# Loading the own probabilities in rows, and moving the second half of the sort matrices behind the first scores

## The chip, the core and the metric

The kernel runs on one core of one Trainium2 chip. The core has a matrix engine (PE; its weight loads are listed apart as PEld), a vector engine (DVE), a scalar engine (ACT), a general engine (POOL) and a sync engine (SP) that mostly issues transfers. Each engine works through its own list of instructions in order and waits on semaphores for the others. Transfers are carried by 16 shared DMA engines; this kernel issues them from SP's queue and from POOL's. PE writes its results to PSUM, from which DVE and ACT copy them into SBUF.

The metric is the device time of one execution in microseconds (us), as the median of several runs. A profile is one more execution, recorded instruction by instruction.

## The reference

Two stages are computed, one after the other. The first is Sinkhorn attention, with 4 batches, 8 heads, 768 tokens, head size 64, and 8 blocks of 96 tokens:

```python
P = sort_net                                  # (4, 8, 8, 8)
for _ in range(5):
    P = exp(P - max(P)); P = P / sum(P, rows); P = P / sum(P, columns)
k_sorted = einsum('bhij,bhjcd->bhicd', P, k in 8 blocks)     # v likewise
attn = softmax(q_block @ k_sorted_block.T / 8)               # within each block
x = attn @ v_sorted_block                                    # (3072, 512)
```

The second is a mixture of 4 experts over all 3072 rows, each row weighted by its own normalized probabilities:

```python
p = domain_probs / (domain_probs.sum(-1) + 1e-9)             # (3072, 4)
out = sum over e of p[:, e] * (relu(x @ w1[e]) @ w2[e])      # 512 -> 1024 -> 512
```

## The kernel before

The order of every engine's instructions is the order in which the program writes them down (a manual schedule), with planned slots later on. PSUM is handed out from two pools of two buffers each, `psM` and `psA`; a tile taken from a pool waits until the tile two takes earlier in that pool has been read.

The start goes like this. SP issues three transfers: `sn` (the sort logits), `p_in` (all probabilities) and `p_own` (the probabilities of the first 768 rows, as 128 partitions x 6 x 4, L171). POOL issues the first half of the queries, k and v of the first four heads and then of the other four, the first expert's first weights, builds the identity matrix `ident`, and some masks and constants. PE multiplies a dummy tile 84 times (`warm`, L276), so that its clock rises. DVE and ACT run the five Sinkhorn steps (L310 to L321), which are serial. In the fifth step PE transposes the first query halves (L288) and does 30 more dummy products.

The last step (L330) writes the sort matrices as `sn16` in two halves, output blocks 0 to 3 on DVE and 4 to 7 on POOL. `r_half(0)` (L342) spreads the first half over 128 partitions into the PSUM tile `ps_R` by four small products, and `build_PI0` (L353) multiplies it by a mask into patterns, four heads an instruction. With these, `mix_half` (L521) sorts and transposes k, or v, of the first batch; before its first use eight dummy products are made (`keep_warm`, L507). `mixed` (L532) copies the result out of PSUM, two blocks at a time. `h_s` multiplies queries by sorted keys and takes the exponential on ACT (L576, L582); `h_w` transposes sorted v (L548, L553); `h_a` is the product with v and the division (L593, L606, L607); `h_x` turns that into the experts' input `xT` (L624, L628); `group0` is the first expert's first layer (L704, L717). `r_half(1)` spreads the second half of the sort matrices, and the copy at L1402 puts both halves into `Rs`, from which POOL builds the patterns of the second half (`build_PI0(nc.gpsimd, 1, ...)`) and later those of the other batches. The relevant order is:

```python
mk0 = mix_half("k", 0, 0, psm, 8)
mixed("k", 0, mk0, 0, 2, act)
mv0 = mix_half("v", 0, 0, psa)
mixed("v", 0, mv0, 0, 2, vec)
r_half(1)
act(Rs.rearrange("p g (a i) -> p a g i", a=2), Rv.rearrange("p a i g -> p a g i"))
h_s(0, 0)
```

Here `vec` and `act` are the copies of DVE and of ACT. Somewhat later the second halves of k and v are mixed (`h_k`, `h_v`), each with one copy of 128 x 768 elements. `own_weights` (L263 to L266) normalizes `p_own` into `p_sb`, which weighs the first expert's output. `room` is a large tile that lies unused until the first expert's second layer.

From about 19 us the experts' products follow one another on PE, with the attention of the next batch in the slots between.

Of the kernel before, what the change touches and what calls it, by code (L numbers as in the profile page):

```python
# [10 lines left out]
F32 = mybir.dt.float32  # L11
# [7 lines left out]
def kernel(  # L19
# [11 lines left out]
    nc = tc.nc  # L31

    B, H, S, D = q.shape
# [4 lines left out]
    E = moe_w1.shape[0]  # L38
    FF = moe_w1.shape[2]
    P = 128  # L40
# [3 lines left out]
    R = BLK // CP  # L44
# [23 lines left out]
    def psa(shape, dtype, name):  # L68
        state["n"] += 1
        return psA.tile(shape, dtype, tag="ps", name=name)  # L70

    def psm(shape, dtype, name):
        return psM.tile(shape, dtype, tag="ps", name=name)
# [27 lines left out]
    room = const.tile([P, 4, Dm], F32, name="room")  # L101
# [5 lines left out]
    def load_natural(b, nm, qd, parts=1, between=None):  # L107
        src = {"k": k, "v": v}[nm]
        t = arena[:, ds(("k", "v").index(nm) * 2 * NW + qd * NW, NW)].rearrange("p (h r d) -> p h r d", h=4, r=R)
        natural[(b, nm, qd)] = t  # L110
        n = 4 // parts
        for m in range(0, 4, n):
            nc.gpsimd.dma_start(
                t[:, ds(m, n)].rearrange("p h r d -> p h (r d)"),
                src[b, ds(4 * qd + m, n)].rearrange("h (p r) d -> p h (r d)", r=R),
            )
            if m == 0 and between:
                between()
# [9 lines left out]
    def head(b, nm, h):  # L128
        return natural[(b, nm, h // 4)][:, h % 4, :, :]
# [20 lines left out]
    def load_half_queries(hf):  # L150
        for qd in range(2):
            nc.gpsimd.dma_start(
                q0[ds(64 * qd, 64), hf].rearrange("p h r d -> p h (r d)"), half_queries(qd, hf)
            )
# [7 lines left out]
    def p_part(at, n):  # L162
        return Tt[2].rearrange("p a f x -> p (a f x)")[:, ds(2 * at, 2 * n)].bitcast(F32)
# [4 lines left out]
    p_own = p_part(2 * E * NT + NT, R * E).rearrange("p (t e) -> p t e", e=E)  # L168
    own_den = p_part(2 * E * NT + NT + R * E, R).rearrange("p (t o) -> p t o", o=1)
    nc.sync.dma_start(p_in, moe_domain_probs.rearrange("(p t) e -> p t e", t=NT))  # L170
    nc.sync.dma_start(p_own, moe_domain_probs[0:S].rearrange("(t p) e -> p t e", p=P))  # L171
    load_half_queries(0)
    load_natural(0, "k", 0)


    ident = const.tile([P, P], F16, name="ident")
    make_identity(nc, ident)
    load_natural(0, "v", 0)
    load_natural(0, "k", 1)
    load_natural(0, "v", 1)  # L180
# [91 lines left out]
    def warm(n):  # L272
        ps = psM.tile([P, 4, P], F32, tag="ps", name=f"ps_w_{state['n']}")
        state["n"] += 1
        for m in range(n):
            nc.tensor.matmul(ps[:, m % 4, :], dummy, dummy, start=True, stop=True)  # L276
# [3 lines left out]
    def h_q(qd, hf, copy, ps=None):  # L280

        if ps is None:
            ps = psa([P, 2, R, 64], F16, f"ps_q_{qd}_{hf}")
        rows = ds(64 * qd, 64)
        for sg in range(2):
            for r in range(R):
                for hh in range(2):
                    nc.tensor.transpose(  # L288
                        ps[ds(D * hh, D), sg, r, :], q0[rows, hf, 2 * sg + hh, r, :], ident[rows, rows]
                    )  # L290
        if copy:
            copy(qT0[qd][:, :, hf], ps[:])
# [16 lines left out]
    for it in range(5):  # L309
        nc.scalar.activation(sn[:], sn[:], AF.Exp, bias=0.0, scale=1.0)  # L310
        if it == 4:
            for qd in range(2):
                h_q(qd, 0, nc.scalar.copy)
            warm(30)
        nc.vector.tensor_reduce(srow[:], sn[:], AX.X, ALU.add)
        nc.vector.reciprocal(srow[:], srow[:])
        nc.vector.tensor_tensor(sn[:], sn[:], srow[:].broadcast_to([GH, NB, NB]), ALU.mult)
        nc.vector.tensor_reduce(scol[:], sn[:].rearrange("p i j -> p j i"), AX.X, ALU.add)
        nc.vector.reciprocal(scol[:], scol[:])
        if it < 4:  # L320
            nc.vector.tensor_tensor(  # L321
                sn[:], sn[:],
                scol[:].rearrange("p j o -> p o j").broadcast_to([GH, NB, NB]),
                ALU.mult,
            )
            if it:
                next(p_steps)

    for a, eng in enumerate((nc.vector, nc.gpsimd)):
# [4 lines left out]
            ALU.mult,  # L334
        )

    ps_R = psM.tile([P, 2, 512], F32, tag="ps", name="ps_R")
    Rv = ps_R[:, :, 0:HB * GH].rearrange("p a (i g) -> p a i g", g=GH)

    def r_half(a):  # L340
        for i in range(HB):
            nc.tensor.matmul(  # L342
                Rv[:, a, i, :], sn16[:, a * HB + i, :, :].rearrange("g j c -> g (j c)"),
                ident[0:GH, 0:GH], start=True, stop=True,
            )
# [4 lines left out]
    Rs = const.tile([P, GH, NB], F16, name="Rs")  # L350

    def build_PI0(eng, a, h0, hn, src):
        eng.tensor_tensor(  # L353
            PI0[a][:, ds(h0, hn)],
            maskk[:, 0:HB * CP].rearrange("p (o i c) -> p o i c", o=1, c=CP).broadcast_to([P, hn, HB, CP]),
            src.rearrange("p g (i o) -> p g i o", o=1).broadcast_to([P, hn, HB, CP]),
            ALU.mult,
        )
# [18 lines left out]
            )  # L377

    r_half(0)
    for h0 in range(0, H, 4):  # L380
        build_PI0(nc.vector, 0, h0, 4, Rv[:, 0, :, ds(h0, 4)].rearrange("p i g -> p g i"))
    vec, act = nc.vector.tensor_copy, nc.scalar.copy


# [119 lines left out]
    def keep_warm(ps, n):  # L504

        for _ in range(n):
            nc.tensor.matmul(ps, dummy, dummy, start=True, stop=True)  # L507
# [3 lines left out]
    def mix_half(nm, qd, hf, pool, warm_up=0):  # L511

        ps = pool([P, 1024], F32, f"ps_m{nm}_{qd}_{hf}")
        keep_warm(ps[:, 0:P], warm_up)
        tails[(nm, qd, hf)] = ps[:, 2 * R * 64:1024].bitcast(F16).rearrange("p (n x) -> p n x", n=2)
        ps = ps[:, 0:2 * R * 64].rearrange("p (s r x) -> p s r x", s=2, r=R)
        for sg in range(2):
            for r in range(R):
                for hh in range(2):
                    h = 4 * qd + 2 * sg + hh  # L520
                    nc.tensor.matmul(  # L521
                        ps[ds(D * hh, D), sg, r, :],
                        head(0, nm, h)[:, r, :],
                        PI0[hf][:, h, :, :].rearrange("p i c -> p (i c)"),
                        start=True, stop=True,
                    )
        return ps

    def mixed(nm, qd, ps, i0, n, copy):

        dst = kTs[qd][:, 0:S] if nm == "k" else vT0[qd]
        copy(  # L532
            dst.rearrange("p (i x c) -> p x i c", i=HB, c=CP)[:, :, ds(i0, n)],
            ps.rearrange("p s r (i c) -> p (s r) i c", c=CP)[:, :, ds(i0, n)],
        )

    def h_k(qd, hf, copy, pool=psa):
        mixed("k", qd, mix_half("k", qd, hf, pool), 0, HB, copy)
# [27 lines left out]
    def h_s(qd, qq, ps=None):  # L566

        kT, ET = kTs[qd], ETs[2 * qd + qq % 2]
        if ps is None:
            ps = psa([P, 2, 512], F32, f"ps_s0_{qd}_{qq}")  # L570
        for n in range(4):
            for hh in range(2):
                sg, i = n // 2, 2 * (qq % 2) + n % 2

                m = BLK if 2 * i + sg == 3 else P
                nc.tensor.matmul(  # L576
                    ps[0:m, hh, ds(n * BLK, BLK)],
                    kT[ds(D * hh, D), ds((2 * i + sg) * BLK, m)],
                    qT0[qd][ds(D * hh, D), sg, qq // 2, :, ds((2 * (qq % 2) + n % 2) * CP, CP)],
                    start=True, stop=True,  # L580
                )
        nc.scalar.activation(  # L582
            ET[:, 0:S].rearrange("c (h x) -> c h x", h=2), ps[0:BLK, :, 0:HS],
            AF.Exp, bias=0.0, scale=SCALE,
        )
# [808 lines left out]
    ]  # L1394


    mk0 = mix_half("k", 0, 0, psm, 8)
    mixed("k", 0, mk0, 0, 2, act)
    mv0 = mix_half("v", 0, 0, psa)
    mixed("v", 0, mv0, 0, 2, vec)  # L1400
    r_half(1)
    act(Rs.rearrange("p g (a i) -> p a g i", a=2), Rv.rearrange("p a i g -> p a g i"))  # L1402
    h_s(0, 0)
    mixed("k", 0, mk0, 2, 2, act)
    load_half_queries(1)
    load_w2(0, 2)
# [33 lines left out]
    evacuate00()  # L1440
    group0(0, 1, 1, [2, 3])
    h_a(1, 1, ps_s11)
    h_k(0, 1, act)
    group0(1, 1, 0, [0, 1])
    h_x(1, vec, [1], ps_s11)
    group0(1, 1, 1, [0, 1])
# [131 lines left out]
```

## Time and profile before

| what | value |
|---|---|
| median of 3 runs | 358.63 us (358.15 to 358.74) |
| profiled execution, its own time | 358.21 us |
| span of that execution, first to last instruction | 356.3 us |
| PE busy | 350.4 us (98%) |
| DVE busy | 277.5 us (78%) |
| ACT busy | 170.1 us (48%) |
| POOL busy | 137.6 us (39%) |
| idle time of PE in the whole span | 5.9 us |
| granted clock of PE | 1.000, mean over the span |

Times in the profile count from the first instruction. A line such as L521 is a line of the kernel before; in the changed kernel the same code stands 3 to 9 lines further down. In lists of instructions "x24" is a count, "out<-in" names the tiles, "128x256" is partitions by elements, and the square brackets tell how long the engine sat idle before and who ended that. The chain that ended last gives start, length, and what it was.

### The profile page before, as it was taken

To read this page: it belongs to the slowest core of one execution; us is meant where nothing else is said; L and a number is where in the kernel's file an instruction comes from. 1 tells how busy PE (TensorE), PEld (TensorE's weight loads), DVE (VectorE), ACT (ScalarE), POOL (GpSimd) and SP (SyncE) were. 2 spreads that over 40 slices of the span, in tenths; PEclk is the share of its full clock that TensorE was granted. 3 is DMA by queue.
4 is the path that set the end of the run, shared out by engine and by line. 5 is a ranking of instruction groups with operands and counts; after the bars stand their busy time and mean duration, and the time that the engine had idled before them with its cause. 6 is when DMAs were issued, how large, how long until landed. Compare 5 with 4: busy or idle time off the path is not lost.

```text
span 356.3 us, 9511 instructions
## 1 busy us (share of the span) xinstructions
PE 350.4 (98%) x3948; PEld 305.5 (86%) x3948; DVE 277.5 (78%) x555; ACT 170.1 (48%) x302; POOL 137.6 (39%) x154
## 2 busy tenths in 40 slices
PE   8899999999999999999999999999999999999996
PEld 8686857888888888988899888888888888888886
DVE  5766787779798687778879988896678886588963
ACT  2653330452425445368847259830288611598301
POOL 8766112466022420000626318840068800188400
PEclk9999999999999999999999999999999999999999
DMA  8999999999999999743995410005200014100021
GB/s 104 203 205 230 212 209 194 207 195 167 195 180 166 195 116 203 138 88 44 180 205 91 107 74 0 2 1 136 78 26 3 2 37 141 62 0 2 0 75 46
DMA packets 74762, 40.26 MB, mean 113 GB/s; under 512 B 41568, under 2 KB 70496, under 8 KB 74720
## 3 DMA queue, kind: packets, MB, share of 16 engines
q0 software_dynamic: 38720, 19.93, 43.2%
q1 hardware_dynamic: 35856, 19.67, 27.2%
q8 instruction: 31, 0.51, 0.6%
q14 instruction: 11, 0.09, 0.1%
q10 hardware_dynamic: 144, 0.07, 0.1%
HBM read 41.88 MB, written 6.34 MB: 135 GB/s over the span
## 4 chain that ended last, share of the span: by engine, by line
PE 95%; DVE 3%; issue 0%; DMA 0%; ACT 0%; DVEq 0%
PE ps_h L815 18%; PE ps_Q L1296 18%; PE ps_p L799 12%; PE ps_X L1153 10%; PE ps_Z L1153 7%; PE ps_Q L1153 7%; PE ps_Z L1296 6%; PE ps_h L704 3%; PE ps_o L741 3%; PE ps_p L860 3%; PE ps_a L479 2%; PE ps_s L444 2%; PE ps_k L425 1%; PE ps_v L391 1%; PE ps_mv L521 1%; PE ps_a L593 0%
## 5 line engine op out<-in xcount | busy, mean ns | idle before, releaser
L815 PE MATMUL ps_h<-xT,w 128*128 128x256 f16 x576 | 67.5, 273 | 0.0
L815 PEld LDWEIGHTS <-w 128*128 128x128 f16 x576 | 55.2, 98 | 7.3
L821 DVE SCALAR_TENSOR_TENSOR Hb<-ps_h,pb 128x1024 f16<-128x1024 f32 x34 | 41.5, 1223 | 17.8 <-PE ps_h L815 17.6
L1153 PEld LDWEIGHTS <-w 128*128 128x128 f16 x480 | 43.6, 98 | 4.7
L1166 POOL TENSOR_TENSOR arena<-tmp,pb 128x512 f16<-128x512 f32 x12 | 15.2, 1276 | 65.7 <-PE ps_Z L1153 49.8
L1296 PEld LDWEIGHTS <-Hb 128*128 128x128 f16 x320 | 31.1, 98 | 3.5
L1165 ACT ACTIVATE tmp<-tmp 128x512 f32<-128x512 f32 x46 | 29.0, 632 | 3.9 <-DVE tmp L1203 3.9
L1296 PEld LDWEIGHTS <-Sb 128*128 128x128 f16 x304 | 28.2, 98 | 3.0
L1153 PEld LDWEIGHTS <-arena 128*128 128x128 f16 x312 | 27.7, 98 | 2.8
L451 ACT ACTIVATE ET<-ps_s 96x768 f16<-96x768 f32 x24 | 18.1, 802 | 25.2 <-PE ps_s L444 25.0
L434 ACT CAST kT<-ps_k 64x384 f16<-64x384 f32 x48 | 22.7, 473 | 13.3 <-PE ps_k L425 12.3
L126 POOL DMA_DIRECT2D arena<-in_q_dram x24 | 19.9, 842 | 20.8 <-DMA q_ring<-arena 17.7
L1153 PE MATMUL ps_X<-ET,arena 128*128 128x256 f16 x168 | 25.2, 272 | 0.0
L1296 PE MATMUL ps_Q<-w,Hb 128*128 128x256 f16 x192 | 24.6, 273 | 0.0
L799 PEld LDWEIGHTS <-Hb 128*128 128x128 f16 x232 | 21.9, 98 | 3.0
L1159 DVE SCALAR_TENSOR_TENSOR Hb<-ps_X,pb 128x512 f16<-128x512 f32 x27 | 18.7, 692 | 7.0 <-PE ps_X L1153 7.0
L1173 ACT COPY ps_X<-ps_Z 128x512 f32<-128x512 f32 x27 | 15.4, 571 | 17.8 <-PE ps_Z L1153 17.8
L1153 PE MATMUL ps_Z<-xT,w 128*128 128x256 f16 (+1 forms) x176 | 22.5, 258 | 0.0
L785 DVE TENSOR_TENSOR Sb<-Hb 128x512 f16<-128x512 f16 x33 | 20.6, 646 | 0.0
L1180 ACT COPY tmp<-ps_X 128x512 f32<-128x512 f32 x26 | 15.2, 586 | 9.2 <-PE ps_X L1153 6.6
L1159 DVE SCALAR_TENSOR_TENSOR Hb<-ps_Z,pb 128x512 f16<-128x512 f32 x27 | 18.4, 683 | 1.3 <-PE ps_Z L1153 1.3
L1203 DVE TENSOR_TENSOR tmp<-ps_Q,tmp 128x512 f32<-128x512 f32 x26 | 17.7, 683 | 0.8 <-PE ps_Q L1153 0.8
(270 smaller groups left out, 744.3 us busy)
## 6 DMA issues: line engine op xcount, KB each, us to landing
w<-in_moe_w_dram POOLq DMA_DIRECT2D x4, 1024.0 KB, 27.2
w<-in_moe_w_dram POOLq DMA_DIRECT2D x6, 512.0 KB, 19.7
arena<-in_k_dram POOLq DMA_DIRECT2D x7, 384.0 KB, 7.6
arena<-in_v_dram POOLq DMA_DIRECT2D x7, 384.0 KB, 8.1
vs<-arena SPq DMA_DIRECT2D x36, 66.0 KB, 5.3
arena<-in_q_dram POOLq DMA_DIRECT2D x24, 96.0 KB, 7.5
out_dram<-ob SPq DMA_DIRECT2D x9, 256.0 KB, 2.0
pb<-p_dram SPq DMA_DIRECT2D x4, 512.0 KB, 5.8
```

The lines of the kernel that those rows point to most:

```text
L126: nc.gpsimd.dma_start(t[:, h // 2, :, h % 2, :], q[b, h].rearrange("(t p) d -> p t d", p=P))
L434: nc.scalar.copy(kT[ds(D * hh, D), r], pk[ds(D * r, D), hh].rearrange("p a (i c) -> p a i c", c=CP),)
L451: nc.scalar.activation(ETs[2 * (pr % 2) + hh][:, 0:S].rearrange("c (a x) -> c a x", a=2), pss[hh][0:BLK, :, 0:HS], AF.Exp, bias=0.0, scale ...
L785: tt(sm[0], blk(0, 1), blk(1, 1), ALU.add)
L799: nc.tensor.matmul(ps, lhs(e, f), Ts[e][rhs][:, f, :], start=(first and e == es[0] and f == 0), stop=(done and e == es[-1] and f == KH - 1 ...
L815: nc.tensor.matmul(ps[:, f, :], w1sb[e][:, kc, ds((4 * g + f) * P, P)], xT[:, kc, ds(2 * c * P, 2 * P)], start=(kc == 0), stop=(kc == NKC ...
L821: nc.vector.scalar_tensor_tensor(out=Hb[:, homes.get(e, e), ds(4 * g, 4), :], in0=ps[:], scalar=0.0, op0=ALU.max, in1=weights(e).broadcast ...
L1153: nc.tensor.matmul(dst[:, ds(f * cols, cols)], a[lhs][:, k, ds((f0 + f) * P, P)], t[rhs][:, k, :], start=(first and f == 0 and k == 0), st ...
L1159: nc.vector.scalar_tensor_tensor(out=home(i, j), in0=src.rearrange("p (f x) -> p f x", f=m), scalar=0.0, op0=ALU.max, in1=weight(j).broadc ...
L1165: nc.scalar.activation(src, src, AF.Relu, bias=0.0, scale=1.0)
L1203: tt(t12, Q, u2, ALU.add)
L1296: nc.tensor.matmul(ps, lhs(e, f), Ts[e][rhs][:, f, part], start=(first and e == 0 and f == 0), stop=(e == E - 1 and f == KH - 1), skip_gro ...
```

## The change

There are six edits.

1. The own probabilities come in as they lie in memory: 6 rows of 128 x 4 values, in six partitions of `room`. A 6x6 float32 identity is copied on POOL, ahead of the second load of `load_natural`. Four float32 products, one for each expert, turn the rows into the layout of `p_own`, and DVE copies them there.
2. The dummy products in the fifth Sinkhorn step are 14 instead of 30.
3. The first patterns are built in three instructions, of 2, 2 and 4 heads, instead of two of 4.
4. The dummy products ahead of the first mix are 4 instead of 8.
5. `h_s(0, 0)` comes ahead of `r_half(1)`, and the copy into `Rs` runs on DVE instead of ACT.
6. The second half of k of the first four heads is copied on ACT in three pieces, of 2, 1 and 1 blocks.

```diff
-    nc.sync.dma_start(p_own, moe_domain_probs[0:S].rearrange("(t p) e -> p t e", p=P))
+    own_rows = room[0:R, 1, :].rearrange("t (p e) -> t p e", e=E)
+    nc.sync.dma_start(own_rows, moe_domain_probs[0:S].rearrange("(t p) e -> t p e", p=P))
     load_half_queries(0)
     load_natural(0, "k", 0)
...
     make_identity(nc, ident)
+    ident32 = room[0:R, 0, 0:R]
+    nc.gpsimd.tensor_copy(ident32, ident[0:R, 0:R])
     load_natural(0, "v", 0)
...
-            warm(30)
+            warm(14)
...
+    ps_own = psm([P, E, R], F32, "ps_own")
+    for e in range(E):
+        nc.tensor.matmul(ps_own[:, e, :], own_rows[:, :, e], ident32, start=True, stop=True)
+    nc.vector.tensor_copy(p_own.rearrange("p t e -> p e t"), ps_own[:])
     ps_R = psM.tile([P, 2, 512], F32, tag="ps", name="ps_R")
...
     r_half(0)
-    for h0 in range(0, H, 4):
-        build_PI0(nc.vector, 0, h0, 4, Rv[:, 0, :, ds(h0, 4)].rearrange("p i g -> p g i"))
+    for h0, n in ((0, 2), (2, 2), (4, 4)):
+        build_PI0(nc.vector, 0, h0, n, Rv[:, 0, :, ds(h0, n)].rearrange("p i g -> p g i"))
...
-    mk0 = mix_half("k", 0, 0, psm, 8)
+    mk0 = mix_half("k", 0, 0, psm, 4)
     mixed("k", 0, mk0, 0, 2, act)
     mv0 = mix_half("v", 0, 0, psa)
     mixed("v", 0, mv0, 0, 2, vec)
+    h_s(0, 0)
     r_half(1)
-    act(Rs.rearrange("p g (a i) -> p a g i", a=2), Rv.rearrange("p a i g -> p a g i"))
-    h_s(0, 0)
+    vec(Rs.rearrange("p g (a i) -> p a g i", a=2), Rv.rearrange("p a i g -> p a g i"))
...
-    h_k(0, 1, act)
+    mk01 = mix_half("k", 0, 1, psa)
+    for i, n in ((0, 2), (2, 1), (3, 1)):
+        mixed("k", 0, mk01, i, n, act)
```

## The prediction

> **What bounds the kernel now.** I read the page's part 1 first (who is busy), then the chain of work that ended last (what the busy engine is made of and where it is not PE), then the timeline of the first 20 us, because every edit lies before 27 us. Page, part 1 and part 4:
>
> ```profile
> PE 350.4 (98%) x3948; PEld 305.5 (86%) x3948; DVE 277.5 (78%) x555; ACT 170.1 (48%) x302; POOL 137.6 (39%) x154
> ...
> PE 95%; DVE 3%; issue 0%; DMA 0%; ACT 0%; DVEq 0%
> ```
>
> PE is busy 350.4 of 356.3 us; the chain has 3% of DVE, and that is the start. Chain, first 45 us:
>
> ```profile
> 10.86 0.69 DVE sn L330
> 11.60 0.26 PE ps_R L342 x4
> 11.86 0.55 PE ps_mk L507 x8
> 12.45 0.57 PE ps_mk L521 x24
> 13.01 0.39 PE ps_mv L521 x24
> 13.43 0.57 DVE Sb L532
> 14.04 0.44 PE ps_mv L548 x4
> 14.57 0.42 DVE Sb L553
> 14.99 0.47 DVE Sb L532
> 15.51 0.42 PE ps_s L548 x4
> 15.94 0.28 PE ps_s L576 x8
> 16.21 0.52 PE ps_mv L521 x24
> 18.77 0.66 PE ps_h L704 x8
> ```
>
> Up to 11.6 us the serial Sinkhorn steps set the time, and the change leaves them alone. From 11.6 to 18.8 us PE and DVE pass one small piece to each other. From 18.77 on PE follows PE, so what is gained by then is kept unless a load is late. Timeline, what the moved parts cost today:
>
> ```profile
> 11.23 1.23 POOL L330 TENSOR_TENSOR sn<-sn,scol 32x512 f16<-32x512 f32 x1
> 11.97 0.75 DVE L353 TENSOR_TENSOR Sb<-maskk,ps_R 128x256 f16<-128x256 f16 x2 [0.43 <-PE ps_R L342]
> 13.65 0.37 ACT L1402 CAST Rs<-ps_R 128x256 f16<-128x256 f32 x1
> 13.97 0.81 ACT L582 ACTIVATE ET<-ps_s 96x768 f16<-96x768 f32 x1
> 14.57 0.42 DVE L553 COPY Sb<-ps_mv 96x512 f16<-96x512 f16 x1 [0.59 <-PE ps_mv L548]
> ```
>
> The last line matters most: DVE idles 0.59 us there, between 13.99 and 14.57.
>
> **1. Own probabilities in rows.** The third DMA on SP's queue keeps its place; it changes from 768 packets of 16 B (6 x 128 rows) to 6 rows of 2 KB. From 2.6 to 5.1 us the small packets share the engines with the first query halves (transfer queues of that stretch: packets, MB, share of 16 engines):
>
> ```profile
> q0 software_dynamic: 361, 0.27, 72.0%
> q1 hardware_dynamic: 794, 0.02, 25.7%
> ```
>
> So q1 takes 25.7% of 2.5 us, 0.64 us at most. The POOL loads reach 130 packets per half microsecond alone and 76, 127 and 98 in the three halves from 3.5 us: 89 packets short, 0.34 us, of which the first half is also ramp; without it 0.14 us. The landing events put k0 at 10.28, v0 at 12.25, k1 at 14.16 and v1 at 16.10 us, and v1's product starts its weights at 16.14. That load is as late as the chain. I take 0.14 us earlier landings (bounds 0 and 0.34): enough to let the chain advance, nothing by itself. The four w1_0 parts land at 17.44, 18.69, 19.94 and 21.42 and are used at 18.58, 19.93, 21.00 and 21.80, so they hold nothing if PE comes 0.14 earlier.
>
> On POOL a 6x6 copy now stands ahead of v0, k1, v1, w1_0, the masks, the memsets and the second half of L330. Nearest rows: a 128x48 memset 0.16, a 128x128 copy 0.29; I take 0.2. The loads behind it wait in a full queue (v0 is issued at 4.13 and starts to move about 8.5), so they lose nothing; L330 ends at 12.66 instead of 12.46, needed about 13.6 (step 3).
>
> On PE 16 warm-ups go (the 30 took 1.85 us, 62 ns each: 0.99 us) and four fp32 products come, each one instruction that loads its own weights. No fp32 product is in the trace. Below: L342's four small ones, 0.26 us together. Above: weights and product in series, 4 x (98 + 219 ns) = 1.27 us. I take 1.0, nearer to the end whose weights also have 128 columns. PE is then free at 8.51 + 14 x 0.062 + 1.0 = 10.4, 1.2 us before L330's first half ends at 11.55: cost nothing. On DVE a 128x24 copy follows L330; a 96x8 reciprocal takes 0.20, a 128x24 one 0.28. It fits the 0.43 us for which DVE waits on ps_R. No gain or loss.
>
> The Trainium skill ("FP8 and Floating Point Precision", TensorE Precision Notes) has true fp32 take four passes; by the 62 ns row that would be an estimate of 16 x 0.062 = 0.99 us, the same cover; no run here shows it.
>
> **2. First patterns in three, four warm-ups fewer.** Two 128x256 instructions of 0.417 us start 0.33 us apart; the first k product starts at 12.45, 0.06 after the first ends. With two heads 128 elements go, at that spacing's slope about 0.14 us (bounds 0.10 and 0.22): product at 12.31. The second piece starts 0.2 later and ends at 12.45; the 12 products before it take 12 x 16 ns, so they barely wait. The extra instruction costs DVE about 0.07 us, before the v copy that waits until 13.29. Keeping eight warm-ups would have held PE to 12.41; four end at 12.18. Gain 0.14.
>
> **3. Second half behind the first scores, its copy on DVE.** Today r_half(1) runs at 13.33 and the scores at 13.59, released by ACT's k copy (13.53). With step 2 that copy ends at 13.39, scores 13.44, r_half(1) ends 13.94, L548 at 13.90: nothing queued behind it is late, as it ends weights by 13.8. ACT loses a 0.37 us copy; the exponential starts at 13.82 instead of 13.97. DVE gets the copy: 128x384 takes 0.56 and 128x256 thus about 0.43 (bounds 0.37, 0.56), from 13.98 to 14.41. L553 behind it is ready at 14.43. Price 0 (bounds 0 and 0.13), covered by the 0.59 us idle. Reader of the sums on POOL: L353 at 17.16, which waited for its own queue until then.
>
> **4. k's second half copied in three.** One ACT copy of 0.82 us becomes 0.48 + 2 x about 0.31 = 1.10 (from 0.48 for 384 and 0.82 for 768 elements: 0.14 fixed). It ends at 24.9; ACT then idles 1.69 us until 26.32, PE refills that bank at 26.21. Price nothing.
>
> **Sum.** 0.14 us off the profiled execution (358.21: span 356.3 and 1.9 around it), 358.07. The median, 358.63, lies 0.42 above it; I carry the difference over: 358.49.
>
> **The rivals.**
> - *More than the sum (faster).* The 0.42 of the median may be v1 landing later than in the profiled execution, and go with the small packets; with step 2 at its upper bound 0.22 and landings 0.34 earlier, and 0.1 for executions where the clock rises late and 30 warm-ups overrun 11.55: 358.63 - 0.22 - 0.34 - 0.1 to - 0.42 - 0.22 - 0.1, 357.97 to 357.89. For it: the coincidence 16.10/16.14. Against: no wait on DMA is left on PE in this execution.
> - *The clock drops (slower).* PE's windows of 3.41 us counted from the rise of the clock at 5.04:
>
> ```profile
> 8.45:11.86 3.41, 2.17 (x46) 1.93 (x38) 2.71 (x11) 1.62 (x3) 3.19 (x16) 1.00 1.28 195
> 353.19:356.30 3.11, 0.24 (x5) 0.07 (x2) 0.29 (x1) 0.00 (x0) 0.00 (x0) 1.00 0.36 126
> ```
>
> The columns are length, then PE, PEld, DVE, ACT, POOL. 64% busy kept the clock full; after the last window with 7% it fell at 356.6. The change leaves 2.17 - 0.99 + 0.26 to 1.27 = 1.4 to 2.4 us, 42 to 72%, between the two. If it falls at 11.86 for one window, the chain's PE pieces of 0.57, 0.39 and 0.44 stretch by the ratio of warm-up spacings before and after 5.04 (96 to 54 ns): 1.40 x 0.78 = 1.1 us, 359.6. It decides if the limit lies above what is left. The Trainium skill ("TensorE: Matmul & The Clock Gate", Part 1) has the clock fall after an idle window of about 3.4 us; by that rule the gap of 1.2 us changes nothing.
> - *The fp32 products run long (slower).* Four passes each in series, 16 x 0.32 = 5.1 us, would end at 14.5. It decides above 2.2 us in all (0.54 each); at 0.8 each PE is 1.0 late: 359.5. Nothing in the trace speaks for it but the missing separate weight loads.
> - *DVE late in step 3.* The copy at 0.56 and r_half(1) 0.15 later: 0.28 lost, 0.14 gained, 358.8.
>
> **How the numbers follow.** Forecast 0.56 (own range 358.1 to 358.8), faster rival 0.19, DVE late 0.07, clock 0.10, fp32 0.08. A change under 0.2% (0.72 us) can hardly be told from none here. The forecast and the late DVE give same 0.63; the faster rival, counted as past the bound, 0.19; the two slower ones 0.18. The range goes from 357.85 to 359.3, which leaves out most of the two slower ones.
>
> **What would show it.** The k product's start (12.45) 0.14 earlier; ps_own done well before 11.5; the Rs copy on DVE inside the idle time before L553; v1's product before 16.1; full clock from 5 us on. Wrong if r_half(0) starts after 11.6, if 128x128 products in the first 16 us take twice their time, or if v1's load holds PE.

## The result and the profile after

The changed kernel takes 359.95 us (median; 359.11 to 360.87, 8 runs) against 358.45 us of the kernel before in the same comparison (358.04 to 359.75, 8 runs): a ratio of 1.004, 95% interval 1.0025 to 1.0055. It is slower, by 1.5 us. The forecast was 358.49 us, with a range of 357.85 to 359.3. The profiled execution took 360.01 us.

The page of the kernel after: the span, busy times, the row of the granted clock (tenths of full speed in 40 slices of 9 us) and the shares of the chain.

```profile
span 358.0 us, 9493 instructions
...
PE 353.0 (99%) x3936; PEld 307.7 (86%) x3936; DVE 278.3 (78%) x558; ACT 169.9 (47%) x303; POOL 137.8 (38%) x155
...
PEclk9699999999999999999999999999999999999999
...
PE 95%; DVE 3%; DMA 0%; issue 0%; ACT 0%; DVEq 0%
```

PE is busy 2.6 us longer with twelve instructions fewer. Part of that is the new fp32 products (2.03 us, for dummies that took less); the rest is products that have become slower, not more. The second digit of the clock is a 6. The windows of 3.41 us, counted from the rise of the clock at 4.79 us, say where (columns: length, then busy time and instructions of PE, PEld, DVE, ACT and POOL, the granted clock, the transfers' share, GB/s):

```profile
4.79:8.20 3.41, 3.41 (x93) 3.31 (x93) 2.83 (x14) 0.51 (x2) 3.41 (x6) 1.00 1.19 159
8.20:11.62 3.42, 3.11 (x40) 2.88 (x32) 2.97 (x13) 1.62 (x3) 3.20 (x16) 1.00 1.24 178
11.62:15.03 3.41, 3.24 (x71) 2.75 (x72) 1.91 (x7) 1.00 (x2) 3.01 (x4) 0.50 1.30 201
15.03:18.44 3.41, 3.41 (x74) 2.85 (x73) 1.94 (x6) 2.26 (x4) 2.45 (x3) 0.50 1.24 206
```

The clock is at half for two windows, 11.62 to 18.44 us, exactly the stretch in which PE and DVE hand each other small pieces. The window before the fall has rows on PE for 3.11 of 3.42 us. What these rows are, PE and DVE show in the timeline of the kernel after:

```profile
8.40 0.95 PE L279 MATMUL ps_w<-Hb 128*128 128x128 f16 x14
9.28 2.03 PE L342 MATMUL ps_own<-room 6*128 6x6 f32 x8
11.66 0.19 DVE L343 COPY T<-ps_own 128x24 f32<-128x24 f32 x1
11.79 0.28 PE L349 MATMUL ps_R<-ident,sn 32*128 32x32 f16 x4 [0.48 <-DVE sn L333]
```

The fourteen dummies, and then the fp32 products: each of the four is recorded as two loads and two products, 2.03 us in all. They end at 11.31, before the sort matrices are there, so nothing waits for them. The chain of the kernel after, from the first sort product on:

```profile
11.79 0.28 PE ps_R L349 x4
12.07 0.54 PE ps_mk L514 x4
12.61 0.78 PE ps_mk L528 x13
13.39 0.64 PE ps_mv L528 x12
...
14.69 0.66 PE ps_mv L555 x4
15.35 0.78 PE ps_mk L528 x12
```

Before, the same pieces were 0.57 (k), 0.39 (v) and 0.44 (the transposes of sorted v, now L555). Marks along the two timelines, us:

| mark (start) | before | after | stretch before | stretch after |
|---|---|---|---|---|
| `r_half(0)` | 11.60 | 11.79 | | |
| first product of `group0` | 18.61 | 20.25 | 7.01 | 8.46 |
| first product of the second layer (`ps_o`) | 27.76 | 29.82 | 9.15 | 9.57 |
| first product of the next first layer (L815) | 36.83 | 38.58 | 9.07 | 8.76 |
| span | 356.3 | 358.0 | | |

So there are two losses, 1.45 us in the stretch at half clock and 0.42 us in the stretch after it, and differences of 0.2 to 0.3 us in the other two (the start and the last stretch), which the experiments below put down to no edit.

### The profile page after: what moved, and what is told of

Its sections match the earlier page's. It is cut to its first block, busy times and chain, and to the rows that moved or that the text cites. A ratio compares the mean times of both kernels' runs of the same rounds, so it can differ in the third digit from the quotient of the medians.

```text
span 358.0 us, 9493 instructions
## 1 busy us (share of the span) xinstructions
PE 353.0 (99%) x3936; PEld 307.7 (86%) x3936; DVE 278.3 (78%) x558; ACT 169.9 (47%) x303; POOL 137.8 (38%) x155
## 4 chain that ended last, share of the span: by engine, by line
PE 95%; DVE 3%; DMA 0%; issue 0%; ACT 0%; DVEq 0%
PE ps_h L822 18%; PE ps_Q L1303 18%; PE ps_p L806 12%; PE ps_X L1160 10%; PE ps_Z L1160 7%; PE ps_Q L1160 7%; PE ps_Z L1303 6%; PE ps_o L748 3%; PE ps_h L711 3%; PE ps_p L867 3%; PE ps_a L486 2%; PE ps_s L451 2%; PE ps_k L432 1%; PE ps_v L398 1%; PE ps_mk L528 1%; PE ps_mv L528 1%
```

## The experiments

The clock's mean over the span counts the windows lost: one window of 3.41 us at half clock is 3.41 / 356.3 / 2 = 0.005 of the mean, so 0.995, 0.99 and 0.986 are one, two and three. The eight executions of the kernel after lost one (359.11, 359.25, 359.55), two (359.9, 360.01, 360.02) or three (360.79, 360.87). None kept the clock.

### Are the sixteen dummies the cause?

Two theories. Clock: the sixteen dummies that go kept the clock up; the kernel before without them is as slow. Path: the fp32 products, the reordering or the copies hold the chain. Four kernels separate them. The changed kernel with thirty dummies:

```diff
-            warm(14)
+            warm(30)
```

> The changed kernel with the 30 dummy products of the kernel before in place of 14; all else as changed. Theory (the clock): the window before 11.6 us has enough products that count, so the mean granted clock goes back to about 1.000; but dummies (1.85 us) and the four float32 products (2.03 us) together end near 12.3 us, so r_half(0) starts 0.5 to 0.7 us late: about 359.0 us, 0.1 to 0.2% over the kernel before. Rival (the float32 products, or edits 3 to 6, cost the time themselves): the clock does not matter, and the time is that of the changed kernel plus 0.5 us or more, 360.4.

The kernel before with fourteen:

```diff
-            warm(30)
+            warm(14)
```

> The kernel before with 14 dummy products in the fifth Sinkhorn step instead of 30, nothing else. Theory (the clock): the 16 missing dummies are what let the clock drop, so it drops here too for one to three windows in most executions (mean clock 0.986 to 0.995): 359.3 to 360.0 us. Rival (the float32 products cause the loss): the clock stays at 1.000 and the time at 358.4.

The changed kernel without edits 1 and 2:

```diff
-    own_rows = room[0:R, 1, :].rearrange("t (p e) -> t p e", e=E)
-    nc.sync.dma_start(own_rows, moe_domain_probs[0:S].rearrange("(t p) e -> t p e", p=P))
+    nc.sync.dma_start(p_own, moe_domain_probs[0:S].rearrange("(t p) e -> p t e", p=P))
...
-    nc.gpsimd.tensor_copy(ident32, ident[0:R, 0:R])
...
-            warm(14)
+            warm(30)
...
-        nc.tensor.matmul(ps_own[:, e, :], own_rows[:, :, e], ident32, start=True, stop=True)
-    nc.vector.tensor_copy(p_own.rearrange("p t e -> p e t"), ps_own[:])
```

> The changed kernel with the own probabilities loaded as before, no float32 products, and 30 dummies: edits 3 to 6 alone. Theory (the clock alone makes the loss): clock 1.000, and the 0.14 us of the prediction's sum is gained, 358.3 us, at most 0.1% off. Rival (the moved copy on DVE or the three pieces cost the time): 358.8 us or more with a full clock.

And edits 1 and 2 alone, on the kernel before, which are these lines the other way round, with 14 dummies:

> The kernel before with edits 1 and 2 alone: rows, float32 products, 14 dummies. Theory (the clock): the whole loss is here, clock 0.986 to 0.995, 359.5 to 360.3 us. Rival (edits 3 to 6): 358.4 to 358.7 us at a full clock.

Measured, beside 358.15 us of the kernel before (34 runs, 33 of them at full clock with a median of 358.13):

| kernel | median us | ratio, 95% interval | executions with 0, 1, 2, 3 windows lost |
|---|---|---|---|
| changed, thirty dummies | 359.58 | 1.0042 (1.0017 to 1.0067) | 6, 4, 2, 0 |
| before, fourteen dummies | 359.36 | 1.0035 (1.002 to 1.005) | 0, 6, 2, 4 |
| edits 3 to 6, thirty dummies | 359.16 | 1.0032 (1.0011 to 1.0052) | 9, 3, 0, 0 |
| edits 1 and 2 | 359.65 | 1.0039 (1.0024 to 1.0053) | 0, 6, 2, 3 |

The second row is the main finding. One number changed, 30 to 14, every execution lost full clock, and the kernel before became as slow as the changed one: the interval holds the changed kernel's 1.004. Its executions also price a window: 358.13 with none, then medians of 358.94, 359.77 and 360.63 with one, two and three, so 0.81 to 0.86 us a window. The windows of that kernel from the rise of its clock:

```profile
5.75:9.16 3.41, 3.41 (x96) 3.26 (x95) 2.67 (x15) 0.51 (x2) 3.41 (x6) 1.00 1.17 152
9.16:12.58 3.42, 1.39 (x24) 1.09 (x22) 2.67 (x11) 1.62 (x3) 3.20 (x14) 1.00 1.26 192
12.58:15.99 3.41, 3.37 (x88) 3.00 (x88) 1.33 (x5) 1.98 (x4) 2.19 (x5) 0.50 1.29 203
```

With 1.39 us of rows on PE (41%) the next window is at half. Edits 1 and 2 add 2 us of fp32 products to the same fourteen dummies, and still all eleven executions fell: these products do not keep the clock.

At equal numbers of lost windows the changed kernel (359.25, 360.01, 360.83) lies 0.2 to 0.3 us above the kernel before with fourteen dummies. That is all that the other edits add to the missing dummies, which are enough by themselves for the other 1.2 us of the median. They are enough, but not the only way to lose the clock, for two rows missed their expectations. With the thirty back the changed kernel still lost windows in half of its executions; the last two runs take that up. And edits 3 to 6 lost a window in 3 of 12, where full clock was expected; their nine executions at full clock have a median of 358.68, with three of them between 360.06 and 361.85, for which no run has a cause.

### The smaller edits, at full clock

Four kernels stand on the kernel before: edits 3 and 4, edit 5, and edits 3, 5 and 6 with 30 and with 46 dummies. Only the first of them has four warm-ups ahead of the first mix, the others eight. Edits 3 and 4:

```diff
-    for h0 in range(0, H, 4):
-        build_PI0(nc.vector, 0, h0, 4, Rv[:, 0, :, ds(h0, 4)].rearrange("p i g -> p g i"))
+    for h0, n in ((0, 2), (2, 2), (4, 4)):
+        build_PI0(nc.vector, 0, h0, n, Rv[:, 0, :, ds(h0, n)].rearrange("p i g -> p g i"))
...
-    mk0 = mix_half("k", 0, 0, psm, 8)
+    mk0 = mix_half("k", 0, 0, psm, 4)
```

> The kernel before with edits 3 and 4 alone: patterns in 2, 2 and 4 heads, 4 dummies ahead of the first k product instead of 8; 30 dummies in the fifth step. Theory (the clock counts products that fill the array): with 4 dummies fewer some executions lose a window of the clock, as in edits 3 to 6 together (3 of 12 at 0.995 there); best time 358.0 or a little below, median 358.4 to 358.8. Rival (edit 5 or 6 is what loses): clock 1.000 throughout, median 358.0 to 358.2.

Edit 5:

```diff
+    h_s(0, 0)
     r_half(1)
-    act(Rs.rearrange("p g (a i) -> p a g i", a=2), Rv.rearrange("p a i g -> p a g i"))
-    h_s(0, 0)
+    vec(Rs.rearrange("p g (a i) -> p a g i", a=2), Rv.rearrange("p a i g -> p a g i"))
```

> The kernel before with edit 5 alone: first scores ahead of r_half(1), the copy into Rs on DVE; 8 and 30 dummies. Theory (the clock, with edit 4 as the reason for what edits 3 to 6 lose): no difference, 358.0 to 358.2 us, clock 1.000. Rival (DVE's copy holds the product behind it): 358.4 us or more at a full clock.

Edits 3, 5 and 6 together:

> Edits 3, 5 and 6 with 8 and 30 dummies as before. Theory (the clock): no lost windows, and of the 0.14 us only what eight dummies leave (they end at 12.41 in the kernel before, the first pattern would be ready at 12.31): 358.0 to 358.15 us. Rival (the order or the three pieces cost time themselves): 358.4 us or more, with slow executions at a full clock.

The same with 46 dummies:

```diff
-            warm(30)
+            warm(46)
```

> As the edits 3, 5 and 6, with 46 dummies in the fifth step instead of 30, so that they fill the time until the sort matrices are ready (8.5 + 46 x 0.062 = 11.35 us). Theory (the clock): the window that the change emptied is fuller than before; no execution loses a window, the slowest lie nearer to the fastest, median 358.0 to 358.1 us. Rival (dummies overrun in executions whose clock rises late): median 358.3 us or more.

| kernel | median us (before: 358.36) | ratio, 95% interval | windows lost |
|---|---|---|---|
| edits 3 and 4 | 358.28 | 1.0008 (0.9992 to 1.0025) | in 2 of 12 |
| edit 5 | 358.61 | 1.001 (0.9999 to 1.002) | in none of 12 |
| edits 3, 5 and 6 | 358.41 | 1.0003 (0.9991 to 1.0015) | in 1 of 11 |
| edits 3, 5 and 6, 46 dummies | 360.49 | 1.0058 (1.0039 to 1.0077) | in none of 6 |

The kernel before itself lies 0.2 us higher here than in the first comparison, so the expectations, given in microseconds, are best read by the ratios.

Edit 3 does what it is for: the first k product starts 0.72 us after `r_half(0)` instead of 0.85, and `group0` 6.89 us after it instead of 7.01. A gain of 0.12 us is under what the time can tell. Edit 4 adds little to it: with edits 3, 5 and 6 and all eight dummies the k product starts 0.74 us after `r_half(0)`.

Edit 5 has a wait that the prediction did not name. Chain of the kernel with edit 5 alone:

```profile
14.14 0.21 PE ps_R L342 x4
14.35 0.02 issue
14.37 0.44 DVE Rs L1403
14.81 0.04 issue
14.85 0.57 PE ps_mk L521 x24
15.42 0.36 PE ps_a L593 x8
```

The second mix of k takes the PSUM buffer of `ps_R`, so it does not start before DVE has copied `ps_R` (14.81, start at 14.85). It starts 3.04 us after `r_half(0)`, before 2.80. Some of the 0.24 us is made up at the next waits: the first product of `group0` comes 7.06 us after `r_half(0)`, before 7.01.

The last row missed its expectation by 2 us at full clock, although the dummies did not delay `r_half(0)` (11.82). In its profile PE waits for nothing that the profile shows ("issue") at two places; these waits from 15 to 50 us:

```profile
PE ps_w L548 <- issue: 0.9, 1, 0.9
PE ps_a L593 <- issue: 0.3, 1, 0.3
```

Between 150 and 200 us PE also waits 0.8 and 0.4 us for loads. The kernel before has no such wait of PE above 0.2 us in its profile. With 22 dummies in place of 30 (below) there was one "issue" of 0.60 us at 14.1. But with edits 3, 5 and 6 and 30 dummies, a list of PE as long as before, there was one too, of 0.57 us at 13.92, in an execution of 359.23 us. So the length alone does not decide. Counted in the traces, all these waits lie at the same places of PE's list: ahead of its 224th product (these two kernels, and edit 1 alone, below), its 352nd (46 dummies, and edit 1 alone) and its 608th (46 dummies, and the changed kernel with 30 and 8). An edit changes which product stands there; what is late was not settled, nor why most executions profiled show no such wait.

### Where the 0.42 us after the half clock come from

The stretch from `group0` to `ps_o` takes 9.15 or 9.16 us in the kernel before and with edits 3 and 4, with edit 5, with fourteen dummies and with edits 1 and 2, but 9.34 to 9.38 with edits 3, 5 and 6 (with or without edit 4, and with 46 dummies), and 9.56 to 9.58 in the changed kernel, with whatever dummies. Edit 6 is in all the long ones. So is something else: one, two or three more instructions in DVE's list (edits 1, 3 and 5 add one each). Two kernels separate these, edits 3 and 5 without 6, and edit 6 alone:

> The kernel before with edits 3 and 5 alone: first patterns in three pieces, r_half(1) behind h_s(0, 0) with its copy on DVE; thirty and eight warm-ups and the single k copy of before stay, so DVE has two more instructions ahead of the second layer stage and edit 6 is absent. Theory A (edit 6 lengthens the stage from the first group0 product to ps_o): the stage is 9.15 us as before; the time is that of the kernel before plus 0.25 for edit 5 less about 0.1 for edit 3, 358.2 to 358.4. Theory B (the stage is lengthened by DVE falling short of instructions at a fixed place of its list, and every extra DVE instruction moves the shortfall onto a later operation): 9.34 to 9.38, with DVE's xsl copy late for the softmax-weighted products; 358.4 to 358.7. The clock is kept by both.

```diff
-    h_k(0, 1, act)
+    mk01 = mix_half("k", 0, 1, psa)
+    for i, n in ((0, 2), (2, 1), (3, 1)):
+        mixed("k", 0, mk01, i, n, act)
```

> The kernel before with edit 6 alone: k's second half copied by ACT in three pieces. DVE's list of instructions is that of before. Theory A: the stage from the first group0 product to ps_o is 9.34 us or more, and the time is 0.2 longer. Theory B: the stage is 9.15 us and the time that of the kernel before within 0.1. The clock is kept by both.

Edits 3 and 5: stretch 9.36 us; 358.89 us against 358.37 (1.0011, 1.0 to 1.0021). Edit 6 alone: 9.16 us; 358.63 us (1.0012, 0.9994 to 1.003). (The execution profiled with edits 3 and 5 lost full clock at 196 us, long after the stretch read here.) By the stretch theory B holds: edit 6 is free there, and the loss follows the number of DVE instructions. By the times it is less clear. Both lie 0.2 us above B's expectation, and for edit 6 alone that is as near to theory A, though the interval includes no change at all. In its profile PE's products are not late: they end at 353.36 us, before at 353.44. What is longer, by 0.4 us, is the end of the span behind them, where only the last outputs are written. DVE's own rows, first with edit 6 alone (none added), then with edits 3 and 5 (two added), then in the changed kernel (three added):

```profile
23.25 0.20 DVE L606 RECIPROCAL rz<-ps_a 96x8 f32<-96x8 f32 x1 [1.24 <-PE ps_a L593]
23.49 0.69 DVE L607 TENSOR_TENSOR xsl<-ps_a,rz 96x512 f16<-96x512 f32 x1
```

```profile
23.39 0.20 DVE L606 RECIPROCAL rz<-ps_a 96x8 f32<-96x8 f32 x1 [1.02 <-PE ps_a L593]
23.84 0.69 DVE L607 TENSOR_TENSOR xsl<-ps_a,rz 96x512 f16<-96x512 f32 x1 [0.24 <-DVE rz L606]
```

```profile
25.08 0.20 DVE L613 RECIPROCAL rz<-ps_a 96x8 f32<-96x8 f32 x1 [1.56 <-PE ps_mk L528]
25.32 0.69 DVE L614 TENSOR_TENSOR xsl<-ps_a,rz 96x512 f16<-96x512 f32 x1
```

With two more, DVE sits idle 0.24 us ahead of `xsl`, whose inputs are ready; the usual gap is 0.04. With three more the gap is one instruction earlier, ahead of `rz`: `ps_a` ended at 24.56 and `rz` starts at 25.08, where before these are 22.92 and 23.02. With none or one more, the same place of the list falls on the copies of `kT` or `xT`, which wait 0.61 and 0.44 us for PE anyway. PE's next products need `xsl` and wait (0.24 us, and their weights 0.47 us, in the changed kernel). The row of the changed kernel names PE's `ps_mk` as what ended the wait. `rz` does not read it, and with 30 and 8 warm-ups (below) `rz` starts at 25.914 us, just ahead of that product's signal at 25.916: the name is a coincidence. What holds in all seven kernels with two or three more instructions is the place: the late one is the 64th of DVE's records in the trace, whatever it computes. That the gap is a late fetch of instructions is an inference from this fixed place; the trace does not name it. Edit 1 alone does not fit the groups by its number, 9.45 us with one more instruction, but there PE itself sits idle for 0.42 us ("issue") within the stretch.

### Where the limit of the clock lies, and whether edit 3 alone pays

> The kernel before with edit 3 alone and six warm-ups ahead of the k product where before has eight and after four (the thirty stay). With the clock by counted activity, the two more than in the earlier run of edits 3 and 4 keep the clock in more executions; the first k product starts 0.7 to 0.75 after r_half(0) where before has 0.85. If nothing else is moved: 0.1 us faster than before, 357.95 to 358.25. If the warm-ups hold PE (the rival): equal to before.

> The kernel before with 22 warm-ups instead of 30. With 14 every execution lost full clock for one to three windows, with 30 none did. If the clock falls by a level of counted activity in a window of 3.41 us, 22 lies between: with 1.7 us of counted rows some executions fall and some do not, depending on where the windows begin, and the median is 358.2 to 359.0. If only gaps without any product matter, 22 gives what 30 gives: 358.1 to 358.4 with the clock kept in all. If the limit lies near what 30 give, all fall: 358.9 to 359.3.

Edit 3 with six warm-ups ahead of the mix: 358.35 us against 358.37 (1.0007, 0.9992 to 1.0021), two of twelve executions with windows lost: no gain. The kernel before with 22 dummies: 358.61 us (1.001, 0.9994 to 1.0026); eight executions kept the clock, two lost one window, two lost two. So 14 dummies never hold it, 22 do in two of three, 30 nearly always. This fits a limit that is a level within a window, with the rest decided by how the windows fall on the dummies; the level itself was not measured. But busy time of PE's rows does not measure that level. The execution profiled with edit 3 and six warm-ups fell after a window with 2.14 us (63%), and the kernel before kept the clock with 2.17:

```profile
7.14:10.56 3.42, 2.60 (x79) 2.38 (x78) 2.74 (x14) 1.25 (x4) 3.20 (x8) 1.00 1.22 169
10.56:13.97 3.41, 2.14 (x70) 1.81 (x70) 2.39 (x7) 1.36 (x3) 3.33 (x12) 1.00 1.30 199
13.97:17.38 3.41, 3.30 (x68) 2.75 (x66) 1.89 (x5) 2.39 (x5) 1.51 (x2) 0.50 1.25 207
```

### The rows and the fp32 products by themselves

Left open was why thirty dummies did not give the changed kernel its clock back. All of the change with 30 and 8 warm-ups, and edit 1 alone with 30 and 8:

> The changed kernel with both groups of warm-ups as before, 30 and 8; edits 1, 3, 5 and 6 stay. Theory W (the warm-ups taken away are all of the clock's loss): full clock in at least 11 of 12 executions, and what is left is the price of the later r_half(0) (about 0.5 us, since the fp32 products end at 12.46) and of DVE's three more instructions (up to 0.4 us): 358.9 to 359.2. Theory F (the fp32 products, 2 us in which the matrix engine does hardly any counted work, take part): one or two windows lost in a quarter to a half of the executions, 359.2 to 359.9.

> The kernel before with edit 1 alone: own probabilities in rows, the 6x6 copy, four fp32 products, DVE's copy; 30 and 8 warm-ups as before. The fp32 products then run from about 10.4 to 12.4 us, and r_half(0) starts at 12.3 instead of 11.81. By theory W the clock holds in at least 11 of 12 and the time is 0.4 to 0.6 longer, 358.6 to 358.9. By theory F windows are lost in a quarter or more, 358.9 to 359.5. By the prediction's first step (the products hidden, nothing on the path): 358.3 to 358.5.

The changed kernel with 30 and 8: 360.23 us against 358.42 (1.004, 1.0027 to 1.0053), above what either theory gave; four of five executions kept the clock, with a median of 359.8. Edit 1 alone: 360.31 us (1.005, 1.0034 to 1.0066); four of eight kept it, with a median of 359.29, and four lost one window. That too is above both theories' ranges. PE with edit 1 alone:

```profile
8.42 1.85 PE L279 MATMUL ps_w<-Hb 128*128 128x128 f16 x30
10.19 2.03 PE L342 MATMUL ps_own<-room 6*128 6x6 f32 x8
12.08 0.25 PE L349 MATMUL ps_R<-ident,sn 32*128 32x32 f16 x4
12.51 0.61 PE L514 MATMUL ps_mk<-Hb 128*128 128x128 f16 x8 [0.18 <-DVE T L343]
```

Behind thirty dummies the fp32 products are the last thing to end, and `r_half(0)` starts when they do. The warm-ups ahead of the mix then wait for DVE's copy of `ps_own`, whose PSUM buffer they take over (0.18 us). At full clock edit 1 so costs about 0.9 us (359.29 against 358.42), and it is also enough to lose the clock in half of the executions, with all dummies in place: theory F for the clock, and the path besides; the five executions of the other kernel tell the theories apart no further. Edit 1 thus has to be paid for either way: with thirty dummies on the path, with fourteen at the clock. The price at full clock was under-expected, 0.4 to 0.6 us; the profiled execution (360.13 us) shows two waits of PE for "issue" on top, 0.28 and 0.42 us, and one of 0.7 us for a load between 150 and 200 us. The two kernels had 5 and 8 runs, too few to give the share of lost windows closely.

No version beat the kernel before; the nearest, edits 3 and 4, cannot be told from it.

## Why the prediction was wrong

The step that failed is step 1's "cost nothing" for the sixteen warm-ups that go. It asked whether PE was free in time for `r_half(0)`, and it was. It did not charge what the dummies were for: keeping the clock through the wait for the sort matrices. With fourteen of them the clock fell in every execution, and that alone made the kernel before 1.2 us slower (358.13 to 359.36). The rival "the clock drops" had the mechanism and nearly the price, and got a chance of 0.10.

- *The clock rival.* It came in all 8 executions. Its time, 359.6 for one lost window, was 1.1 us over the forecast; measured is 0.81 to 0.86 us a window, and mostly two or three were lost, hence 359.95. Its price took 96 and 54 ns as the spacings of the warm-ups at half and full clock; in the trace of before they are 107 and 56, which by the same sum would give 1.27 us, further from what a window cost. Its low chance came from a range read as "42 to 72% busy", between 7% (fell) and 64% (kept), counting the fp32 products as activity. The window before the fall was 91% busy by its rows, and fell. Fourteen dummies with the fp32 products fell as often as fourteen without. By the Trainium skill ("TensorE: Matmul & The Clock Gate", Part 1) the clock falls after an idle window. The prediction used that against the rival. The trace does not agree with it as it was read there: no gap in the window of the fall is longer than 0.48 us. What exactly is counted stays open, only that it is not the rows' time.
- *Step 1, fp32 products.* 1.0 us was taken, with 1.27 as the upper bound; 2.03 were measured, outside the bounds. The bound added one load and one product an instruction; the trace shows two of each, 0.25 us a pair. The Trainium skill ("FP8 and Floating Point Precision", TensorE Precision Notes) has four passes for true fp32. The records here show two products and two loads each, and 2.03 us is twice the 0.99 that the prediction estimated from it. With fourteen dummies this cover of 0.43 us was still enough; with thirty it was not. The rival of long fp32 products needed 2.2 us to decide and did not, narrowly.
- *Step 1, landings.* 0.14 us was taken; the runs show nothing of that size. v1 landed at 15.69 to 16.11 us in the five kernels with rows, and at 15.30 to 16.54 in the eleven with the small packets. These ranges cannot tell 0.14 us from none. PE waited for none of these loads in the kernel after.
- *Step 1, POOL's copy, and the start of `r_half(0)`.* The copy took 0.18 us against 0.2 taken. `r_half(0)` at 11.79 instead of 11.60 is no sign of it: in ten kernels whose code up to there is that of before, or differs only in its dummies, it starts between 11.81 and 12.06. The profiled execution of before was an early one; its stretch from `ps_o` to L815, 9.07 us, was in turn 0.3 longer than the 8.76 to 8.78 of most kernels. The base of the sum was therefore as sure as some 0.3 us.
- *Step 2.* Right: 0.13 us against 0.14 forecast, from `r_half(0)` to the k product. It was swallowed by the rest. The reason for edit 4 was wrong: eight warm-ups were to hold PE until 0.81 us after `r_half(0)`, but with them the k product came at 0.74, 0.02 later than with four. And the four warm-ups taken may not be free of charge: with 30 dummies and 4 warm-ups, 2 or 3 of 12 executions lost windows, where the kernel before lost them in 2 of 110.
- *Step 3.* The copy's length (0.42 us for 0.43), its place and the missing price at L553 were right. The wait that mattered was another one: the next mix takes `ps_R`'s buffer. It was sized at 0 and measured 0.24 at that product, 0.05 at `group0`. The time, 1.001 (0.9999 to 1.002), settles no more.
- *Step 4.* Right on PE: edit 6 alone leaves the stretch at 9.16 us, and PE's products end no later.
- *A term that was missing.* DVE is 0.2 to 0.4 us late at a fixed place of its list. Each added instruction moves the list against that place, until one that PE waits for stands there. The prediction charged each instruction only its own duration.

The other two rivals did not come: no execution was faster by more than the scatter, and DVE was not late at L553 (`Rs` ends at 15.15, L560 starts at 15.46 in the kernel after).

## What to carry to other kernels

Dummy products in a wait of PE are worth what the clock is worth in the latency-bound stretch behind them, not the time that they occupy: before taking them away, put that stretch at half clock into the sum. That the profile shows other work in the same slot as busy does not make it a replacement: sixteen more full-width 16-bit products kept the clock here, and four 6x6 fp32 products did not. When an instruction is added or moved, look also at who takes over its PSUM buffer next.

## What was not expected of the hardware

- The clock falls with no idle stretch: after a window in which PE's rows were busy for 3.11 of 3.42 us, 2.03 of them fp32 products of 6x6.
- The loss goes with the number of dummies: with 14 the clock fell in 12 of 12 executions, 22 in 4 of 12, 30 in 2 of 110 (the kernel before in the four comparisons of the experiments).
- A 6x6 fp32 product takes 0.5 us in all, two loads of about 0.32 us and two products of 0.37 us that overlap in part.
- 768 packets of 16 B, or 6 of 2 KB instead, made no difference to any landing that the runs can tell.
- PE and DVE sat idle for 0.2 to 0.9 us, with nothing in the profile to wait for, at fixed places of their lists: ahead of PE's 224th, 352nd or 608th product (0.28 to 0.90 us, in five of sixteen profiles), and ahead of DVE's 64th record (a gap of 0.24 us there with two more instructions, and one 0.42 us longer than before with three).
